# Attention and experts in one kernel: the first expert's early slots filled from six batches instead of seven

## The chip, the core and the metric

The kernel runs on one core of a Trainium2 chip. The metric is the device time of one execution in microseconds (us).

## What is computed

Eight batches of 576 tokens go through block-causal attention (8 heads of 64), and the result, 4608 rows of 512, goes through a mixture of eight experts. Each token is served by the one expert with the largest logit.

```python
scores = where(block(i) >= block(j), q @ k.T / 8, -1e9)
x      = softmax(scores) @ v                  # (8, 8, 576, 64) -> (4608, 512)
logits = x @ w_gate                           # (4608, 8)
e      = argmax(logits); g = softmax(logits)[e]
out[i] = g[i] * (relu(x[i] @ w1[e]) @ w2[e])  # w1: 512 x 1024, w2: 1024 x 512
```

## The kernel before

**Attention.** The work is cut into 32 pairs of heads, four to a batch. Pairs go through a software pipeline: a hand-written string, `ORDER`, lists the steps of one turn, each with a lag, and turn `t` runs step `name:lag` for pair `t - lag`. Scores are made with lag 2, transposes and products with V with lag 3, and with lag 4 the folds `F1`, `F2`, `F0` (L291, L297) that turn the pair's output into rows and gate logits, and the scalings `X1`, `X2` (L305, into the row tile `xt`), `Y1`, `Y2`, `Y0` (L312, L315). The last turn is turn 35, and only pair 31's lag 4 is left in it. Two folds share one PSUM bank, so `F2` needs `X1` and `Y1` done.

**Loads.** SP issues each pair's `qd`, `kd`, `v` (L96 to L98) one turn ahead of GpSimd's scaling `q<-qd` (L104, step `pQ`), which stands on GpSimd ahead of the scaling `p<-p,rs` (L205, step `Z`) of the pair two before it. Each turn PE waits for that `p` at the transpose `pt..t` (L228).

**Routing.** When a batch's four pairs are done, `Router.batch` runs as a generator: at each `z` in `ORDER` one step of it (two for batch 6). It ranks the tokens with matmuls, stores the rows to `xd` in DRAM (`rows`, L512 and L517) and queues in `late` five scatters that write token numbers into the table `tab` (L658). Each `y` of `ORDER`, two to a turn, takes one to four jobs off `late`. Where `late` is empty, a `y` takes a job off `todo` instead: the split of the first expert's w1 into `high` and `low`.

**The hand-over.** Three slots of 128 rows (`EARLY`) of the first expert are filled before routing has ended. After batch 6 the kernel reads the first three columns of the table (`first`, L632) and gathers their rows from `xd` into `xg[0..2]` (L674). `first_slot` then transposes slot 0 (L1207, between `F1` and `F2` of the last turn) and multiplies it with w1 (L1217) beside the rest of the last pair. Batch 7's columns 0 to 383 are stored by `part` as soon as three pairs are scaled, columns 384 to 511 after the last pair.

**Experts.** A critical section (L1026) begins when every transfer under way has landed. In it the engines follow hand-written programs with semaphores. DVE places batch 7's tokens (L649 to L653), prepares weights, and computes in `slots` (L696 to L713) which expert each slot serves; then come `high` (L1047) and `low` (L1053), the split of the weights, and PE's second layer `second_pe` (L934). SP loads the next weights and GpSimd gathers slot 3 (L794, L798) once `slots` is done.

Of the kernel before, what the change touches and what calls it, by code (L numbers as in the profile page):

```python
# [17 lines left out]
P = 128  # L18
# [20 lines left out]
class Attention:  # L39
# [8 lines left out]
    def __init__(self, ctx, tc, ident, qT, kT, vt, w_gate):  # L48
# [19 lines left out]
        self.small_bank, self.at = (None, None), {}  # L68
        self.used = {}
# [233 lines left out]
    def op_X(self, m, n):  # L303
        out = self.out(m // 4)[0][:, 2 * n - 2 : 2 * n, P * (m % 4) : P * (m % 4) + P]
        self.nc.vector.tensor_mul(  # L305
            out.rearrange("p i (j d) -> p i j d", d=D),
            self.rows(m, n)[:, :, 0:P].rearrange("p i (j d) -> p i j d", d=D), self.scaled(m, n, D),
        )

# [41 lines left out]
    def run(self, order, sink, part, other, then):  # L351
# [9 lines left out]
        for turn in range(self.M + last):  # L361
            for name, lag in order:
# [18 lines left out]
                if name[0] in "XY":  # L381
                    left[m // 4] -= 1
                    if left[m // 4] == 5:
                        part(m // 4, self.xs[m // 4][0])
# [51 lines left out]
EARLY = 3  # L436


class Router:
# [6 lines left out]
    def __init__(self, cp, tp, sp, tc, B, xd, tab, ident):  # L446
# [14 lines left out]
        for b in range(B):  # L461
# [28 lines left out]
            for c in range(self.ntok - S, self.ntok + 1, P)  # L490
        ]

        self.sums = [tp.tile([P, 2, E + 4], F32, tag=f"sum{i}", name=f"sum{i}") for i in range(2)]
        for t in self.sums:
            nc.gpsimd.memset(t[:, :, 0:4], 0.0)
        self.meta = {
            k: tp.tile(shape, dt, tag=k, name=k)
            for k, shape, dt in (
                ("cnti", [P, E], I32), ("each", [P, 2, E], I32), ("le", [P, 2, E], F32), ("prod", [P, 3, E], F32),
                ("n", [P, 2], F32), ("s", [P, 3], F32), ("si", [P, 2], I32), ("e8", [P, 1], I32),  # L500
# [5 lines left out]
    def rows(self, b, xt, x0, c0, c1):  # L506
# [12 lines left out]
        if b == self.B - 1:  # L519
            for m in put:  # L520
                self.keep_apart(m, 0)

# [6 lines left out]
    def batch(self, b, xt, x0, lg):  # L529
# [55 lines left out]
        if b >= self.B - 2:  # L585
# [24 lines left out]
        nc.sync.dma_start(self.xd[b * S : b * S + 64, GATE : GATE + 1], g[0:64, 4:5])  # L610
# [17 lines left out]
        if b == self.B - 2:  # L628
# [3 lines left out]
            self.late.append(lambda: nc.sync.dma_start(self.first, self.tabv[:, 0:EARLY]))  # L632
# [24 lines left out]
    def scatter(self, b, i, posi):  # L657
# [8 lines left out]
        if b < self.B - 1:  # L666
            for other in self.scatters:
                self.tc.declare_no_dep(put.ins, other.ins, reason="other rows")
            self.scatters.append(put)
        return put  # L670
# [10 lines left out]

    def next_late(self):

        for _ in self.late[: 1 if len(self.late) <= 5 else 4]:
            self.late.pop(0)()
        if len(self.late) == EARLY + 1:
            self.late.pop(0)()

    def slots(self, cnt, do):
# [3 lines left out]
        cnti, each, le, prod, n, s, si, e8, off, col, row = self.meta.values()  # L693
        a, c = self.sums
# [14 lines left out]
        do(v.tensor_sub(s[:, 0:1], self.part, s[:, 0:1]))  # L709
# [6 lines left out]
class Experts:  # L716
# [9 lines left out]
    def __init__(self, ctx, tc, ident, w1, w2, out, router, high, low):  # L726
# [26 lines left out]
        self.py = [b("py0"), b("py1")]  # L753

# [12 lines left out]
    def run(self):  # L767
# [258 lines left out]
        with tc.tile_critical():  # L1026
# [56 lines left out]
            self.router.slots(cnt, do)  # L1083
# [54 lines left out]
def attention_moe_kernel(ctx, tc, qT, kT, vt, w_gate, w1, w2, out):  # L1138
# [16 lines left out]
    with ExitStack() as actx:  # L1155
# [21 lines left out]
        def sink(b, xt, x0, lg):  # L1177
# [7 lines left out]
            if b == B - 2:  # L1185
# [3 lines left out]
            return router.batch(b, xt, x0, lg), 2 if b == B - 2 else 1  # L1189

        def part(b, xt):
            if b == B - 1:
                router.rows(b, xt, None, 0, 3 * P)
# [54 lines left out]
```

## Time and profile before

| what | value |
|---|---|
| median of three runs | 887.78 us (886.81 to 889.24) |
| the profiled execution, its own time | 886.42 us |
| its span on the core | 884.6 us |
| PE busy in the span | 841.5 us (95%) |
| DVE, ACT, GpSimd busy | 401.7, 459.5, 393.9 us |
| mean granted TensorE clock | 0.986 of full |

The span is counted from the first instruction to the last; some 1.8 us of the profiled execution lie around it. Times in rows are microseconds from the span's start. A turn of attention takes some 11 us, and attention fills the span up to about 387 us.

### The profile page before, as it was taken

How to read it: one execution, taken by the hardware profiler on the slowest of the kernel's cores; microseconds unless marked ns; L12 is line 12 of the kernel's file. 1: busy time of each engine (PE TensorE's matmuls, PEld its weight loads, DVE VectorE, ACT ScalarE, POOL GpSimd, SP SyncE). 2: the span in 40 equal slices, each digit the busy share in tenths (PEclk: the TensorE clock that was granted, in tenths of full speed). 3: DMA queues.
4: the chain of work that ended last, by engine and by line, in shares of the span. 5: the costliest groups of instructions: out<-in, count | busy, mean ns of one | idle time of the engine just before them, and what ended most of it. 6: DMA issues, size and time to landing. Idle time of an engine off the chain costs nothing.

```text
span 884.6 us, 15857 instructions
## 1 busy us (share of the span) xinstructions
PE 841.5 (95%) x4936; PEld 633.7 (72%) x4936; DVE 401.7 (45%) x1142; ACT 459.5 (52%) x1155; POOL 393.9 (45%) x392
## 2 busy tenths in 40 slices
PE   4999999999999999947999999999999999999994
PEld 3666666666666666636888888888888888888882
DVE  3667777767777777519804300045547352000000
ACT  3777777777777777514343443334433444334431
POOL 4122344444444323216655544455656655454541
PEclk9999999999999999979999999999999999999997
DMA  5228526273626261324733411125645531111110
GB/s 188 81 91 183 142 91 167 91 163 95 153 93 147 93 146 53 85 53 146 271 104 90 177 44 49 49 71 181 232 141 159 206 109 49 48 39 34 49 49 28
DMA packets 45043, 98.14 MB, mean 111 GB/s; under 512 B 7517, under 2 KB 10845, under 8 KB 44958
## 3 DMA queue, kind: packets, MB, share of 16 engines
q1 hardware_dynamic: 37438, 77.07, 30.2%
q0 software_dynamic: 7520, 19.97, 6.8%
q8 instruction: 49, 0.80, 0.4%
q14 instruction: 36, 0.29, 0.1%
HBM read 76.76 MB, written 20.79 MB: 110 GB/s over the span
## 4 chain that ended last, share of the span: by engine, by line
PE 89%; DMA 4%; DVE 3%; ACT 1%; issue 1%; POOL 1%; SPq 0%; POOLq 0%; DVEq 0%; ACTq 0%
PE py L934 24%; PE ph L855 22%; PE o L262 11%; PE ya L161 6%; PE xa L161 4%; PE pt L896 4%; PE o L297 3%; DMA xd<-xt 2%; PE px L816 2%; PE o L291 1%; DMA tab<-toks,posi 1%; PE o L150 1%; ACT pb L192 1%; DMA out<-y,idx 1%; DVE rc L651 1%
## 5 line engine op out<-in xcount | busy, mean ns | idle before, releaser
L934 PE MATMUL py<-w,low 128*128 (+1 forms) x912 | 232.9, 405 | 2.6 <-DVE w L1047 2.3
L934 PEld LDWEIGHTS py<-w,low 128*128 128x128 f32 x912 | 167.4, 190 | 38.7 <-DVE w L1047 2.7
L855 PE MATMUL ph<-w,xh 128*128 (+1 forms) x576 | 149.6, 392 | 0.9 <-ACT xf L829 0.9
L104 POOL TENSOR_SCALAR q<-qd 128x640 f32<-128x640 f32 x32 | 57.9, 1810 | 190.6 <-PE o L150 120.1
L1047 DVE CAST w<-raw 128x1024 fp32r<-128x1024 f32 x59 | 49.1, 881 | 193.6 <-PE ph L855 141.3
L855 PEld LDWEIGHTS ph<-w,xh 128*128 128x128 f32 x576 | 108.1, 188 | 24.9 <-ACT xf L829 1.1
L888 ACT ACTIVATE h<-ph 128x512 f32<-128x512 f32 x74 | 44.3, 599 | 146.6 <-PE ph L855 146.6
L916 POOL TENSOR_TENSOR low<-hf,low 128x512 fp32r<-128x512 f32 x74 | 101.1, 1366 | 36.7 <-ACT hf L910 36.7
L835 POOL TENSOR_TENSOR xl<-xf,xh 128x512 fp32r<-128x512 f32 x38 | 50.6, 1332 | 104.0 <-ACT xf L829 103.9
L1053 DVE TENSOR_TENSOR w<-raw,w 128x1024 fp32r<-128x1024 f32 x60 | 80.3, 1399 | 0.0
L855 PE MATMUL ph<-w,xl 128*128 (+1 forms) x288 | 77.5, 391 | 1.3 <-POOL xl L835 1.3
L906 ACT CAST low<-pt 128x512 fp32r<-128x512 f32 x76 | 45.8, 602 | 59.4 <-PE pt L896 56.6
L192 ACT ACTIVATE pb<-ya,neg 128x320 f32<-128x320 f32 (+2 forms) x96 | 50.1, 525 | 48.2 <-DVE neg L177 48.1
L954 POOL DMA_INDIRECT out<-y,idx x35 | 40.0, 1144 | 66.1 <-ACT y L948 66.1
L161 PE MATMUL ya<-kd,q 64*128 64x192 f32 (+2 forms) x192 | 61.8, 457 | 2.7 <-ACT pb L192 2.7
L855 PEld LDWEIGHTS ph<-w,xl 128*128 128x128 f32 x288 | 54.0, 188 | 13.5 <-POOL xl L835 1.7
L948 ACT ACTIVATE y<-py,xg 128x512 f32<-128x512 f32 x38 | 26.2, 689 | 71.8 <-PE py L934 71.8
L161 PE MATMUL yb<-kd,q 64*128 64x192 f32 (+2 forms) x192 | 61.8, 457 | 0.0
L658 POOL DMA_INDIRECT tab<-toks,posi x40 | 42.3, 1058 | 27.0 <-DVE run L625 19.6
L910 ACT COPY hf<-pt 128x512 f32<-128x512 f32 x76 | 46.4, 611 | 8.9 <-POOL low L916 8.6
L192 ACT ACTIVATE pb<-yb,neg 128x192 f32<-128x192 f32 (+2 forms) x96 | 49.8, 526 | 0.2 <-DVE neg L177 0.2
L798 POOL DMA_INDIRECT xg<-xd,idx x37 | 44.1, 1191 | 10.9 <-POOL idx L794 10.9
(937 smaller groups left out, 1641.6 us busy)
## 6 DMA issues: line engine op xcount, KB each, us to landing
raw<-w SPq DMA_DIRECT2D x60, 512.0 KB, 5.5
qd<-qT SPq DMA_DIRECT2D x32, 352.0 KB, 3.2
v<-vt SPq DMA_DIRECT2D x32, 352.0 KB, 4.4
kd<-kT SPq DMA_DIRECT2D x32, 288.0 KB, 3.9
xd<-xt SPq DMA_DIRECT2D x7, 1026.0 KB, 9.4
xg<-w SPq DMA_DIRECT2D x8, 256.0 KB, 8.5
xd<-xg SPq DMA_DIRECT2D x4, 256.5 KB, 12.0
xd<-x SPq DMA_DIRECT2D x8, 128.0 KB, 4.2
```

The source lines that it names most:

```text
L104: self.nc.gpsimd.tensor_scalar(q, self.raws[m][0][:, 0 : 512 + P], 0.125, None, ALU.mult)
L161: ins = mm(out, q[r, 128 * (i - 1) : 128 * i], k[r, o : o + n], start=True, stop=True, skip_group_check=True)
L192: ins = self.nc.scalar.activation(dst, src, AF.Exp, bias=self.neg[m][:, c : c + 1], scale=1.0, accum_out=self.sums[m][:, c : c + 1])
L262: self.nc.tensor.matmul(out[r], self.raws[m][2][:, slot], self.ph[m, bank][:, c0:c1], start=t in (0, 5), stop=t in (4, 5), skip_group_chec ...
L835: pool.tensor_sub(self.xl, self.xf, self.xh).then_inc(sem["xp"], 1)
L855: m = pe.matmul(self.ph[f], x[:, P * k : P * k + P], weights(k, f, part), start=start and k == 0, stop=stop and k == 3,)
L906: act.copy(self.hh[t % 2][:, f], self.pt[f]).then_inc(sem["ha"], 1)
L910: act.copy(self.hf, self.pt[f]).then_inc(sem["ha"], 1)
L916: engine.tensor_sub(self.hl[t % 2][:, f], self.hf, self.hh[t % 2][:, f]).then_inc(sem["hp"], 1)
L934: m = pe.matmul(self.py[t % 2], h[:, c // 4, P * (c % 4) : P * (c % 4) + P], wf[:, bass.ds(off + (base + 512 * c), 512)], start=n == 0, st ...
L1047: copy(hi, raw[m % nr]).then_inc(sem["wh"], 1)
L1053: dve.tensor_sub(lo, raw[m % nr], hi).then_inc(sem["wd"], 1)
```

## The change

Three things are done. **(1)** The early slots take tokens of batches 0 to 5 (`LATE = 2`): the counting matmuls, `lack`, the read of `first` and the three gathers follow batch 5 instead of batch 6. The gathers are declared free of the rows of batches 6 and 7, and the scatters of batch 6 free of the read of `first`. Batch 6 is routed at one step for each `z`. `next_late` takes one job per `y`. Since a slot may point at a row of the last two batches that is not yet written, nine writes of zeros (and one row) go to `xd` after batch 0 instead of four (and 65 rows). What is left of `todo` is issued when batch 5 ends instead of batch 6. **(2)** `X1`, `X2` of the last pair are declared free of the store `part`, which reads other columns of the same tile. **(3)** `slots` keeps its running values in a PSUM bank (`few`) and sums over experts by a product with a triangle of ones and one reduction, in place of three shifted adds in SBUF.

```diff
+LATE = 2
 class Router:
         self.zeros = [
             (xd[c : min(c + P, self.ntok + 1)], self.xg[0][0 : min(P, self.ntok + 1 - c)])
-            for c in range(self.ntok - S, self.ntok + 1, P)
+            for c in range(self.ntok - LATE * S, self.ntok + 1, P)
         ]
...
+        self.upto = tp.tile([P, E, E], F32, tag="upto", name="upto")
+        nc.gpsimd.memset(self.upto, 1.0)
+        nc.gpsimd.affine_select(out=self.upto, in_=self.upto, compare_op=ALU.is_ge, fill=0.0, ...)
...
 def batch(self, b, xt, x0, lg):
-        if b >= self.B - 2:
+        if last or b == self.B - LATE - 1:
             mm(total, self.ones, self.run[:, b], start=True, stop=False, skip_group_check=True)
...
-        if b == self.B - 2:
+        if b == self.B - LATE - 1:
             yield
             c = self.run[:, b + 1, 0:1]
             v.scalar_tensor_tensor(c, lack, float(EARLY), c, ALU.min, ALU.add)
-            self.late.append(lambda: nc.sync.dma_start(self.first, self.tabv[:, 0:EARLY]))
+            self.late.append(self.read_first)
             self.late += [lambda t=t: self.gather(t) for t in range(EARLY)]
...
 def next_late(self):
-        for _ in self.late[: 1 if len(self.late) <= 5 else 4]:
-            self.late.pop(0)()
-        if len(self.late) == EARLY + 1:
-            self.late.pop(0)()
+        self.late.pop(0)()
...
 def op_X(self, m, n):
+        for other in self.stored.get(m, ()):
+            self.tc.declare_no_dep(ins.ins, other.ins, reason="other columns")
...
-    def slots(self, cnt, do):
+    def slots(self, cnt, do, bank):
-        a, c = self.sums
+        a, le = (bank[:, 2 * E * i : 2 * E * i + 2 * E].rearrange("p (a e) -> p a e", a=2) for i in range(2))
+        s = bank[:, 4 * E : 4 * E + 3]
...
-        do(v.tensor_copy(a[:, :, 4:], each))
-        for k in (1, 2, 4):
-            do(v.tensor_add(c[:, :, 4:], a[:, :, 4:], a[:, :, 4 - k : 4 - k + E]))
-            a, c = c, a
-        do(v.tensor_scalar(le, a[:, :, 4:], self.part, None, ALU.is_le))
+        do(v.tensor_copy(a, each))
+        do(v.tensor_mul(sums, a[:, :, None, :].to_broadcast([P, 2, E, E]), self.upto[:, None].to_broadcast([P, 2, E, E])))
+        do(v.tensor_reduce(a, sums, AX.X, ALU.add))
+        do(v.tensor_scalar(le, a, self.part, None, ALU.is_le))
...
-        do(v.tensor_sub(s[:, 0:1], self.part, s[:, 0:1]))
+        do(v.tensor_scalar(s[:, 0:1], s[:, 0:1], self.part, -1.0, ALU.subtract, ALU.mult))
...
 def sink(b, xt, x0, lg):
-            if b == B - 2:
+            if b == B - LATE - 1:
                 while todo:
                     todo.pop(0)()
-            return router.batch(b, xt, x0, lg), 2 if b == B - 2 else 1
+            return router.batch(b, xt, x0, lg), 1
```

How the order of instructions changes on GpSimd at the hand-over, from pair 30's scaling on (`posi5`, `posi6` are batches 5 and 6, `p031` is pair 31's scaling, `sxl` belongs to slot 0). Before:

```order
L205 TENSOR_SCALAR p030_4485<-p030_4485,rs30_4483 128x64
L658 DMA tab_58<-toks_131,posi6_4691 43008x1 x4
L205 TENSOR_SCALAR p031_4618<-p031_4618,rs31_4616 128x64
L658 DMA tab_58<-toks_131,posi6_4691 43008x1
L674 DMA xg0_173<-xd_57,first_172 128x513
L674 DMA xg1_174<-xd_57,first_172 128x513
L674 DMA xg2_175<-xd_57,first_172 128x513
L1210 TENSOR_TENSOR sxl_4851<-oT_4852,sxh_4850 128x512
```

and with the change:

```order
L668 DMA tab_58<-toks_131,posi5_4186 43008x1
L206 TENSOR_SCALAR p030_4488<-p030_4488,rs30_4486 128x64
L686 DMA xg0_173<-xd_57,first_172 128x513
L686 DMA xg1_174<-xd_57,first_172 128x513
L206 TENSOR_SCALAR p031_4631<-p031_4631,rs31_4629 128x64
L686 DMA xg2_175<-xd_57,first_172 128x513
L668 DMA tab_58<-toks_131,posi6_4749 43008x1 x5
L1224 TENSOR_TENSOR sxl_4854<-oT_4855,sxh_4853 128x512
```

Two gathers now stand ahead of pair 31's scaling, and batch 6's five scatters behind the last gather, where four of them stood ahead of that scaling.

The other place is SP's queue after batch 0, where the zeros are written ahead of the first weights (`xg1` to `xg3`) and the loads of pair 8. `DMAHW0` to `DMAHW7` are the semaphores that SP's transfers take in turn: a row that waits for one waits until the transfer eight rows ahead of it has landed. Before:

```order
L1180 DMA xd_57<-xg0_173 128x513 [waits DMAHW3_49]
L1180 DMA xd_57<-xg0_173 128x513 [waits DMAHW4_49]
L1180 DMA xd_57<-xg0_173 128x513 [waits DMAHW5_49]
L1180 DMA xd_57<-xg0_173 128x513 [waits DMAHW6_49]
L1180 DMA xd_57<-xg0_173 65x513 [waits DMAHW7_49]
L1165 DMA xg1_174<-w1 128x512 [waits DMAHW0_49]
L1165 DMA xg2_175<-w1 128x512 [waits DMAHW1_49]
L1165 DMA xg3_176<-w1 128x512 [waits DMAHW2_49]
L96 DMA qd8_904<-qT 128x704 [waits DMAHW3_49,PE_49,Pool_49]
L97 DMA kd8_905<-kT 128x576 [waits DMAHW4_49]
L98 DMA v8_906<-vt 128x704 [waits DMAHW5_49]
```

and with the change, from the sixth write of zeros (five like it stand ahead) on:

```order
L1195 DMA xd_57<-xg0_173 128x513 [waits DMAHW0_49]
L1195 DMA xd_57<-xg0_173 128x513 [waits DMAHW1_49]
L1195 DMA xd_57<-xg0_173 128x513 [waits DMAHW2_49]
L1195 DMA xd_57<-xg0_173 128x513 [waits DMAHW3_49]
L1195 DMA xd_57<-xg0_173 1x513 [waits DMAHW4_49]
L1180 DMA xg1_174<-w1 128x512 [waits DMAHW5_49]
L1180 DMA xg2_175<-w1 128x512 [waits DMAHW6_49]
L1180 DMA xg3_176<-w1 128x512 [waits DMAHW7_49]
L97 DMA qd8_907<-qT 128x704 [waits DMAHW0_49,PE_49,Pool_49]
L98 DMA kd8_908<-kT 128x576 [waits DMAHW1_49]
L99 DMA v8_909<-vt 128x704 [waits DMAHW2_49]
```

Pair 8's loads, which stood behind the first, second and third write of zeros by their semaphores, now stand behind the sixth, seventh and eighth.

## Rows read from the trace of the kernel before

**Rows 1.** Waits of PE over the whole span: us in total, times, longest.

```profile
PE sa L1207 <- DMA xg<-xd,first: 8.0, 1, 8.0
...
PE px L816 <- SPq L1026: 3.5, 1, 3.5
...
PE py L934 <- DVE w L1047: 2.3, 1, 2.3
...
PE pt31t L228 <- POOL p L205: 0.5, 1, 0.5
```

**Rows 2.** The chain that ended last, 370 to 428 us: start, us, what.

```profile
370.80 6.89 DMA tab<-toks,posi
...
380.19 3.33 DMA xg<-xd,first
...
387.75 8.54 DMA xd<-xt
...
424.74 2.81 PE py L934 x12
```

**Rows 3.** PE's timeline: first fold of turn 34, of turn 35, slot 0's transposes.

```profile
367.09 0.66 PE L297 MATMUL o<-fold,oT 128*128 128x144 f32 x4
...
374.82 0.76 PE L297 MATMUL o<-fold,oT 128*128 128x144 f32 x4 [0.57 <-ACT oT L269]
383.56 1.11 PE L1207 MATMUL sa<-ident,xg 128*128 128x128 f32 x4 [7.98 <-DMA xg<-xd,first]
```

**Rows 4.** DVE's timeline: the last scaling of turns 34 and 35, and pair 31's X1.

```profile
370.05 0.29 DVE L312 COPY x<-o 64x144 f32<-64x144 f32 x1
...
377.63 0.43 DVE L305 TENSOR_TENSOR xt<-o,rs 128x256 f32<-128x256 f32 x1 [3.10 <-DMA xd<-xt]
...
386.78 0.29 DVE L312 COPY x<-o 64x144 f32<-64x144 f32 x1
```

**Rows 5.** The page's groups: the scatters on GpSimd, mean ns of one.

```profile
L658 POOL DMA_INDIRECT tab<-toks,posi x40 | 42.3, 1058 | 27.0 <-DVE run L625 19.6
```

**Rows 6.** SP's timeline: when pair 8's qd and v were issued.

```profile
74.39 0.33 SPq L96 DMA_DIRECT2D qd<-qT  x1
...
78.35 0.33 SPq L98 DMA_DIRECT2D v<-vt  x1
```

**Rows 7.** DMA issues of the whole span: KB each, median us to landing.

```profile
qd<-qT SPq DMA_DIRECT2D x32, 352.0 KB, 3.2
```

**Rows 8.** DMA issues between 60 and 82 us: KB each, median us to landing.

```profile
qd<-qT SPq DMA_DIRECT2D x2, 352.0 KB, 5.7
```

**Rows 9.** GpSimd's timeline in turn 9: pair 8's q, pair 6's p.

```profile
85.47 1.81 POOL L104 TENSOR_SCALAR q<-qd 128x640 f32<-128x640 f32 x1 [8.07 <-PE o L150]
88.32 0.44 POOL L205 TENSOR_SCALAR p<-p,rs 128x64 f32<-128x64 f32 x1 [1.04 <-ACT ph6k L243]
```

**Rows 10.** PE's timeline in turn 9: the transpose that needs pair 6's p.

```profile
90.56 0.27 PE L228 MATMUL pt6t<-ident,p 128*64 128x128 f32 x1
```

**Rows 11.** DVE's timeline in and behind `slots`.

```profile
408.35 3.18 DVE L703 TENSOR_SCALAR le<-sum,part 128x16 f32<-128x16 f32 x1
...
412.40 1.12 DVE L708 CAST si<-s 128x2 int32<-128x2 f32 x1
...
414.61 1.90 DVE L1047 CAST w<-raw 128x1024 fp32r<-128x1024 f32 x3
```

**Rows 12.** GpSimd's timeline at the same place.

```profile
410.20 1.29 POOL L916 TENSOR_TENSOR low<-hf,low 128x512 fp32r<-128x512 f32 x1
412.19 1.29 POOL L916 TENSOR_TENSOR low<-hf,low 128x512 fp32r<-128x512 f32 x1 [0.70 <-ACT hf L910]
...
416.27 1.11 POOL L798 DMA_INDIRECT xg<-xd,idx  x1 [0.32 <-POOL idx L794]
```

**Rows 13.** PE's timeline: the first 24 matmuls of the second layer.

```profile
416.56 7.30 PE L934 MATMUL py<-w,low 128*128 128x512 f32 x24 [2.30 <-DVE w L1047]
```

**Rows 14.** The window 416.5 to 418: busy PE, PEld, DVE, ACT, POOL; PEclk, DMA share, GB/s.

```profile
416.50:418.00 1.50, 1.44 (x3) 1.16 (x4) 1.47 (x3) 0.00 (x0) 0.88 (x1) 0.50 0.87 248
```

More of the change, by code (lines that the diff above doesn't have):

```diff
@@ L383, in run @@
                     if left[m // 4] == 5:
-                        part(m // 4, self.xs[m // 4][0])
+                        self.stored[4 * (m // 4) + 3] = part(m // 4, self.xs[m // 4][0])
                     if left[m // 4] == 0:
@@ L489, in __init__ @@
             (xd[c : min(c + P, self.ntok + 1)], self.xg[0][0 : min(P, self.ntok + 1 - c)])
-            for c in range(self.ntok - S, self.ntok + 1, P)
+            for c in range(self.ntok - LATE * S, self.ntok + 1, P)
         ]
-        self.sums = [tp.tile([P, 2, E + 4], F32, tag=f"sum{i}", name=f"sum{i}") for i in range(2)]
-        for t in self.sums:
-            nc.gpsimd.memset(t[:, :, 0:4], 0.0)
+        self.upto = tp.tile([P, E, E], F32, tag="upto", name="upto")
+        nc.gpsimd.memset(self.upto, 1.0)
+        nc.gpsimd.affine_select(
+            out=self.upto, in_=self.upto, compare_op=ALU.is_ge, fill=0.0, base=0, pattern=[[1, E], [-1, E]],
+            channel_multiplier=0,
+        )
         self.meta = {
@@ L609, in batch @@
         self.rows(b, xt, x0, 0, RW)
[L610 removed]
+        m = nc.sync.dma_start(self.xd[b * S : b * S + 64, GATE : GATE + 1], g[0:64, 4:5])
+        if b >= self.B - LATE:
+            self.keep_apart(m, 0)
         yield
@@ L669, in scatter @@
             self.scatters.append(put)
+            if b >= self.B - LATE:
+                self.tc.declare_no_dep(put.ins, self.closed.ins, reason="other columns")
         return put
@@ L680, in gather, with read_first @@
         self.keep_apart(m, 1)
+    def read_first(self):
+        self.closed = self.nc.sync.dma_start(self.first, self.tabv[:, 0:EARLY])
     def next_late(self):
-        for _ in self.late[: 1 if len(self.late) <= 5 else 4]:
-            self.late.pop(0)()
-        if len(self.late) == EARLY + 1:
-            self.late.pop(0)()
-    def slots(self, cnt, do):
+        self.late.pop(0)()
+    def slots(self, cnt, do, bank):
         v = self.nc.vector
-        cnti, each, le, prod, n, s, si, e8, off, col, row = self.meta.values()
-        a, c = self.sums
+        cnti, each, prod, n, sums, si, e8, off, col, row = self.meta.values()
+        a, le = (bank[:, 2 * E * i : 2 * E * i + 2 * E].rearrange("p (a e) -> p a e", a=2) for i in range(2))
+        s = bank[:, 4 * E : 4 * E + 3]
         do(v.tensor_scalar(cnti, cnt, float(SL - 1), None, ALU.add))
@@ L1082, in run @@
                 dve.tensor_copy(self.w[:, 0, 0, o], self.high[:, o]).then_inc(sem["wh"], 2)
-            self.router.slots(cnt, do)
+            self.router.slots(cnt, do, self.bank)
             dve.sem_inc(sem["me"], 1)
@@ L1184, in sink @@
                 here.append(b)
-            if b == B - 2:
+            if b == B - LATE - 1:
                 while todo:
                     todo.pop(0)()
-            return router.batch(b, xt, x0, lg), 2 if b == B - 2 else 1
+            return router.batch(b, xt, x0, lg), 1
         def part(b, xt):
-            if b == B - 1:
-                router.rows(b, xt, None, 0, 3 * P)
+            return router.rows(b, xt, None, 0, 3 * P) if b == B - 1 else []
         def other():
```

13 lines of the change are left out of this document (8 added, 5 removed).

## The prediction

> **What bounds the kernel now.** I read the page first: PE is busy for 841.5 of 884.6 us, so only what PE waits for can be won or lost. PE's waits come next [rows 1]: the longest by far is 8.0 us in front of slot 0's transposes, on the gather of the first expert's rows; 3.5 us go to the start of the critical section, 2.3 to the weight splits behind `slots`, 0.5 to pair 31's `p`. Third, the chain [rows 2] says what makes that gather late: batch 6's last scatter lands 6.89 us after 370.80, then the table is read, then the gather needs 3.33 us and ends at 383.5. Behind it comes the store of the last columns, 8.54 us from 387.75, and the critical section opens when it lands at 396.29. So two links in a row set the hand-over: routing of batch 6, and the last store.
>
> **Part 1 and 2, the hand-over.** In the last turn the first fold starts at 374.82 and the last scaling, whose end releases the store, ends at 386.78 + 0.29 = 387.07 [rows 3, 4]. The same steps one turn earlier take from 367.09 to 370.34, 3.25 us. The difference, 9.0 us, holds the wait for the gather (7.98), `X1`'s wait for another store (it begins at 377.63 after 3.10 us; the fold was done at 375.6), and transposes and folds at a low clock (1.11 us where the same kind takes 0.66). For the last turn to run like the one before it, both waits must go: with the gather early but `X1` still held until 377.63, only about 7 us would go. By the new order both go: the gather of slot 0 stands behind pair 30's scaling, a turn ahead of its use, and needs 3.33 us; `X1` has no DMA left to wait for.
>
> Batch 6's scatters used to stand ahead of pair 31's `p`, which cost PE 0.5 us [rows 1]; now one gather issue stands between, and I count the 0.5 as won. Together **9.5 us**: the last scaling ends at 377.5, the last store lands at about 386.8.
>
> What is late next? The five scatters now come after pair 31's gather, once batch 6's positions are known, by the order just behind turn 34's second `X2`, some 370.3 [rows 4]. At 1.06 us each with a gap [rows 5] the last is issued near 377 and, at the 6.89 us seen before [rows 2], lands by 384, ahead of the store. They also stand ahead of slot 0's `sxl` on GpSimd, which PE needs only after two groups of matmuls and the ranking. Their price is zero, and up to 3 us if the store's landing is drawn out by them or by batch 6's rows, which now leave a turn's third later, close to `part`. Slot 0's matmuls themselves have cover: PE stood idle for 3.5 us at the critical section [rows 1], so their end is not what it waits for.
>
> Moved work with no price: six tiny counting matmuls go from batch 6 to batch 5; batch 6's routing steps spread over two turns, in which DVE has idle time; the rest of `todo` goes to GpSimd earlier, where it idles more than half of the span; the three declarations cost nothing.
>
> **The zeros.** Nine writes of 256 KB go out where four did, and by the order pair 8's `qd` now waits for the sixth to land instead of the first. Before, `qd` was issued at 74.39 and `v`, two writes on, at 78.35 [rows 6]: 1.98 us for a write. So `qd` is issued at 74.39 + 5 x 1.98 = 84.3, and lands after 3.2 us (the median of all) to 5.7 (in this busy stretch) [rows 7, 8]: 87.5 to 90.0. GpSimd then needs 1.81 us for `q` and 0.44 for `p` [rows 9] behind it in its queue, and PE wants that `p` at 90.56 [rows 10]. It comes at 89.8 to 92.3: a new stall of 0 to 1.8 us in turn 9, which attention, with PE at 100%, never gives back. I take **1.0 us lost**; if the loads also queue behind the last three writes and the first weights, it is up to 5. The `q` itself, `kd` and `v` are used a turn later and stay covered.
>
> **Part 3, `slots`.** The row shows `le`, 16 elements a partition, taking 3.18 us and ending at 411.53, 0.04 us behind GpSimd's `low` (411.49); the cast `si` takes 1.12 us and ends 0.04 behind the next `low` (413.48) [rows 11, 12]. The four steps between them take 0.22 each. So a one-source step from SBUF to SBUF sits out GpSimd's work, and the others don't. With both in PSUM I take 2.96 + 0.90 = 3.9 us off; product and reduction in place of three adds are about even. From `le` on, eleven steps of 0.22 end near 410.8 instead of 414.5.
>
> Then the three casts `high` (0.63 each) meet GpSimd's two `low`: done between 412.7 and 414.8. PE has been free since 416.56 - 2.30 = 414.26 [rows 13], so it starts at 414.3 to 414.8 and wins about 2.1 us. The 24 matmuls took 7.30 us there, where a dozen takes 2.81 [rows 2], because the clock stood at half (0.50) behind the wait [rows 14]; with the wait gone I expect full clock and 5.6 us, so 1.7 more. But then slot 3's rows come due: their gather began at 416.27 [rows 12], 1.8 us behind the end of `slots`, and cannot start much before 413.48 + 1.8 = 415.3, and an early gather landed after 3.33 us [rows 2]; beside the weight loads I allow 5. PE would reach it at 420.1 and gets it at 418.6 to 420.3. I take **2.8 us** won of 3.8, with 0.5 (casts held, clock still falls) and 4 as ends.
>
> Not all of `slots` is freed: `off`, `e8` and `row` still go from SBUF to SBUF. They come at about 410, inside the `low` that ends at 411.49. If they wait, `slots` ends at 412.1 and the casts at 414.0 to 415.4. The Trainium skill ("SBUF — State Buffer", section "SBUF: two separate sides") says that DVE and GpSimd share a pair of ports under an exclusive lock, so that a DVE step in a two-port mode is blocked for a whole GpSimd instruction; "VectorE: DVE Perf Modes", section "Why PSUM operands drop a tier", says that a PSUM operand rules that mode out. The trace agrees for `le` and `si`; by the same rule the three left over would wait, and the sum would win 2.0 there instead of 2.8. No row shows such a step with one element a partition under a GpSimd instruction, so I keep the larger value.
>
> **The sum.** 9.5 - 1.0 + 2.8 = 11.3 us. The profiled execution took 886.42, so 875.1 for one like it; it lies 1.36 below the median of the three runs (887.78), and against that the forecast is **876.5 us**.
>
> **The rivals.**
> - *The zeros cost 5 us.* For it: in the old trace the transfers keep the engines busy until pair 8's loads are in. Against: the spacing of 1.98 us. 876.5 + 4.0 = 880.5. Chance 0.15.
> - *`slots` wins nothing*: the leftovers or the casts wait for GpSimd, or slot 3's gather binds, and the clock falls all the same. 876.5 + 2.3 = 878.8. Chance 0.12.
> - *The last store lands late*, behind `part`, batch 6's rows and five scatters, which were all done before. For it: three transfers now share the stretch; against: the data are small. 876.5 + 3 = 879.5. Chance 0.08.
> - *Slower.* The writes of zeros hold SP's queue so long that turns 9 and 10 run dry. With s us for a write the stall is 74.39 + 5s + 5.7 + 2.25 - 90.56 = 5s - 8.2; the 12.3 us won elsewhere and 2.7 more (0.3%) are used up from s = 4.6. At s = 5 the stall is 16.8, 4.5 us more than is won: 892.3. The trace shows 1.98, so chance 0.02.
> - *An extra slot.* If the first expert had under 384 tokens in batches 0 to 5, padding would make a slot more, some 12 us (468 us from 416.56 to the end, over 38 slots): 888.5, no change. Against: from the reference's inputs it has 192 + 128 + 576 = 896 there. Chance 0.03, with everything else that eats up the whole gain.
>
> **How the numbers follow.** The forecast with its own bounds (872.5 to 879) has 0.60. 0.3% is about what a measurement of this kernel tells from no change, 2.7 us. Faster by more than that: the forecast and the first three rivals, 0.95; within it 0.03; slower 0.02. The range runs from 871.5 (no stall at the zeros, 4 us at `slots`, a point more at the hand-over) to 882 (two of the first three rivals at once).
>
> **What would show it.** Right: no wait of PE at slot 0's transposes and none at the last `pt..t`; critical section opened 9 to 10 us earlier; `le` and `si` near 0.2 us, the second layer's first 24 matmuls in under 6 us; a new wait of PE on `p` in turn 9 of 0 to 2 us. Wrong: a wait for `first` or a gather left on GpSimd ahead of pair 31's `p`; `X1` still ending at a store; the last store landing over 9.5 us after its issue; PE waiting in turns 9 to 11 for loads by more than 5 us.

## The result, and the profile after

The changed kernel takes 880.13 us in the median of eight runs (875.76 to 883.50), the kernel before 887.39 in eight runs beside them (885.07 to 890.53). The ratio is 0.9908, with an interval of 0.9881 to 0.9936: faster by about 1%. A second set of runs gave 874.34 against 885.64, ratio 0.9881 [0.9857, 0.9906] (experiment e1). The execution profiled after, the fastest of its eight, took 875.76 us, with a span of 874.0; the one before took 886.42 and 884.6. The two profiles are 10.6 us of span apart.

PE's waits over the whole span of the changed kernel (us in total, times, longest; beside them stand only those of the first and second turns, two of 0.7 and 0.6 us that are shown further down, and some under 0.7 us that both kernels share):

```profile
PE px L831 <- issue: 4.3, 1, 4.3
...
PE pt6t L229 <- POOL p L206: 2.2, 1, 2.2
...
PE bank L585 <- DVE oh L569: 0.9, 1, 0.9
```

Against [rows 1], the 8.0 us at slot 0's transposes are gone, and so are the 0.5 us on pair 31's `p`; the splits' 2.3 us are 0.7. New are 2.2 us on pair 6's `p`, 0.9 us on the ranking inside slot 0's matmuls, and 0.6 us on slot 3's gather. The wait for the critical section grew from 3.5 to 4.3. Two waits that the kernel before had just behind the section's start, 1.3 us for GpSimd's `xl` and 0.9 us for ACT's `xf`, are gone too.

**The last turn.** PE's and DVE's timeline of the changed kernel (start, us, engine, line, what, idle time ahead and what ended it): first fold, slot 0's transposes, second fold; `X1` and the last scaling:

```profile
376.29 0.76 PE L298 MATMUL o<-fold,oT 128*128 128x144 f32 x4 [0.57 <-ACT oT L270]
376.89 0.60 PE L1221 MATMUL sa<-ident,xg 128*128 128x128 f32 x4
377.76 0.73 PE L298 MATMUL o<-fold,oT 128*128 128x144 f32 x4 [0.27 <-DVE lg L318]
...
377.09 0.42 DVE L306 TENSOR_TENSOR xt<-o,rs 128x256 f32<-128x256 f32 x1 [1.09 <-PE o L298]
...
379.35 0.29 DVE L315 COPY x<-o 64x144 f32<-64x144 f32 x1
```

From the fold to the end of the last scaling it is 3.35 us (376.29 to 379.64), where [rows 3, 4] had 12.25. `X1` now ends its wait at PE's fold, not at a store. GpSimd's timeline shows the gathers that made this possible, the first and second (at 361.60) ahead of pair 31's `p`, and the five scatters of batch 6 behind the third:

```profile
360.26 1.03 POOL L686 DMA_INDIRECT xg<-xd,first  x1 [0.39 <-issue]
...
369.68 0.44 POOL L206 TENSOR_SCALAR p<-p,rs 128x64 f32<-128x64 f32 x1 [7.14 <-ACT ph31b L244]
370.32 1.01 POOL L686 DMA_INDIRECT xg<-xd,first  x1 [0.19 <-issue]
372.85 1.01 POOL L668 DMA_INDIRECT tab<-toks,posi  x1 [1.52 <-DVE run L635]
...
378.05 0.98 POOL L668 DMA_INDIRECT tab<-toks,posi  x1 [0.31 <-issue]
```

In the chain that ended last, the last store is still the link into the critical section, and a little longer than in [rows 2] (8.54):

```profile
380.31 9.03 DMA xd<-xt
```

Only the first part of it is data. For the five microseconds ahead of its landing at 389.34 the DMA engines move nothing (columns: us, busy PE, PEld, DVE, ACT, POOL; PEclk, DMA share, GB/s), and before it was the same from 391 to 396. What fills that time the profiles don't show.

```profile
384.00:389.00 5.00, 2.24 (x10) 1.49 (x8) 0.00 (x0) 0.67 (x2) 0.00 (x0) 1.00 0.00 0
```

**Turn 9.** SP's, GpSimd's and PE's timeline: the zeros, the first weights, pair 8's `qd`; pair 8's `q`, pair 6's `p`, the transpose that wants it.

```profile
65.19 9.58 SPq L1195 DMA_DIRECT2D xd<-xg  x10
75.98 5.53 SPq L1180 DMA_DIRECT2D xg<-w  x3
83.31 0.33 SPq L97 DMA_DIRECT2D qd<-qT  x1
...
90.73 1.81 POOL L105 TENSOR_SCALAR q<-qd 128x640 f32<-128x640 f32 x1 [13.24 <-DVE g L648]
92.52 0.44 POOL L206 TENSOR_SCALAR p<-p,rs 128x64 f32<-128x64 f32 x1
...
93.02 0.30 PE L229 MATMUL pt6t<-ident,p 128*64 128x128 f32 x1 [2.21 <-POOL p L206]
```

`qd` was issued at 74.39 before [rows 6] and goes out 8.9 us later; `q` starts 5.3 us later than in [rows 9]. The DVE step named ahead of `q` was done long before; in e1 the same row begins at 89.37 and names the transfer `qd`.

**Behind the critical section.** PE's timeline: the first transposes, the second layer's first 24 matmuls, slot 3's transposes.

```profile
390.55 1.12 PE L831 MATMUL px<-ident,xg 128*128 128x128 f32 x4 [4.31 <-issue]
...
408.27 5.84 PE L949 MATMUL py<-w,low 128*128 128x512 f32 x24 [0.74 <-DVE w L1062]
...
414.68 0.65 PE L831 MATMUL px<-ident,xg 128*128 128x128 f32 x4 [0.57 <-DMA xg<-xd,idx]
```

Before, the first of these rows stood at 397.46, the last at 423.70. So the 10.6 us divide as 6.91 up to the critical section's first transposes, 2.11 from there to slot 3's (26.24 us became 24.13), and 1.6 in the steady rest, which nothing in the prediction accounts for.

The same place on DVE (`few` is the PSUM bank; then the first and last of the three steps left in SBUF, of 0.15 us each, and the weight splits) and on GpSimd:

```profile
402.76 0.24 DVE L717 TENSOR_SCALAR few<-few,part 128x16 f32<-128x16 f32 x1
...
403.88 0.16 DVE L722 CAST si<-few 128x2 int32<-128x2 f32 x1
...
404.52 0.15 DVE L725 TENSOR_SCALAR off<-si 128x1 int32<-128x1 int32 x1
...
404.90 0.15 DVE L727 TENSOR_SCALAR row<-n 128x1 int32<-128x1 f32 x1
405.20 3.01 DVE L1062 CAST w<-raw 128x1024 fp32r<-128x1024 f32 x3
...
402.24 1.30 POOL L850 TENSOR_TENSOR xl<-xf,xh 128x512 fp32r<-128x512 f32 x1
403.49 1.29 POOL L931 TENSOR_TENSOR low<-hf,low 128x512 fp32r<-128x512 f32 x1
405.47 1.59 POOL L931 TENSOR_TENSOR low<-hf,low 128x512 fp32r<-128x512 f32 x1 [0.69 <-ACT hf L925]
...
408.70 1.65 POOL L813 DMA_INDIRECT xg<-xd,idx  x1 [0.45 <-POOL idx L809]
```

The steps that took 3.18 and 1.12 us [rows 11] take 0.24 and 0.16, and both run while GpSimd works (`xl` and the first `low`). The three splits, which are still held by the second `low`, take 3.01 instead of 1.90.

### The profile page after: what moved, and what is told of

The parts are those of the page before. It is cut to its first block, busy times and chain, and to the rows that moved or that the text cites. A ratio compares the mean times of both kernels' runs of the same rounds, so it can differ in the third digit from the quotient of the medians.

```text
span 874.0 us, 15861 instructions
## 1 busy us (share of the span) xinstructions
PE 838.9 (96%) x4936; PEld 632.9 (72%) x4936; DVE 399.4 (46%) x1141; ACT 459.7 (53%) x1155; POOL 397.1 (45%) x392
## 4 chain that ended last, share of the span: by engine, by line
PE 86%; DMA 5%; issue 2%; POOL 2%; ACT 2%; DVE 1%; SPq 1%; POOLq 0%; DVEq 0%; ACTq 0%
PE py L949 23%; PE ph L870 22%; PE o L263 10%; PE ya L162 6%; PE xa L162 4%; PE pt L911 4%; PE o L298 3%; PE px L831 2%; DMA xd<-xg 2%; PE o L292 1%; DMA xd<-xt 1%; ACT pb L193 1%; DMA qd<-qT 1%; DMA xg<-xd,idx 1%; POOL tab L668 1%
## 5 line engine op out<-in xcount | busy, mean ns | idle before, releaser
L949 PE MATMUL py<-w,low 128*128 (+1 forms) x912 | 229.9, 401 | 0.8 <-DVE w L1062 0.7
L931 POOL TENSOR_TENSOR low<-hf,low 128x512 fp32r<-128x512 f32 x74 | 102.9, 1391 | 35.5 <-ACT hf L925 35.5
L1068 DVE TENSOR_TENSOR w<-raw,w 128x1024 fp32r<-128x1024 f32 x60 | 83.1, 1445 | 0.0
```

What stands on the lines that cost most here:

```text
L931: engine.tensor_sub(self.hl[t % 2][:, f], self.hf, self.hh[t % 2][:, f]).then_inc(sem["hp"], 1)
L949: m = pe.matmul(self.py[t % 2], h[:, c // 4, P * (c % 4) : P * (c % 4) + P], wf[:, bass.ds(off + (base + 512 * c), 512)], start=n == 0, st ...
L1068: dve.tensor_sub(lo, raw[m % nr], hi).then_inc(sem["wd"], 1)
```

## The experiments

Each is compared with runs of the kernel before on the same chip: 885.64 us for e1 to e4, 885.16 for e5 to e8, 885.05 for e9 to e12. Differences between experiments are of medians; between sets they carry the 0.6 us by which the medians of before differ.

**e1, the changed kernel again**, unchanged.

> The changed kernel once more, for a second trace. Theory (what differs between executions lies in the experts' part, whatever the kernel): the third row transpose, slot 3's, starts again at 414.7 us (414 to 415.5), and only the stretch from there to the end differs from the 459.3 us of the first trace, by as much as the execution's own time does. Rival (the change itself is drawn differently each time: the clock at the critical section, the last store, the loads): the slot-3 transposes start 2 us or more away from 414.7 and the stretch behind them stays within 0.7 us of 459.3.

Measured: 874.34 us (872.55 to 877.72), ratio 0.9881 [0.9857, 0.9906]; span 871.0. From slot 3's transposes (411.58) to the end it is 459.4 us, against 459.3 in the first profile: the experts' part does not differ between these two executions, so that theory is wrong (in e3, whose program is the same there, it was 461.2). What differs lies ahead: the wait in turn 9 is 0.9 instead of 2.2 us, the last store takes 8.11 instead of 9.03, and the clock behind the critical section falls later.

**e2, the zeros spread** over batches 0, 1 and 2.

```diff
-            if b == 0:
-                for rows, zero in router.zeros:
-                    nc.sync.dma_start(rows, zero)
+            for rows, zero in router.zeros[4 * b : 4 * b + 4]:
+                nc.sync.dma_start(rows, zero)
+            if b == 0:
```

> The ten writes of zeros go out four after batch 0, four after batch 1, two after batch 2, instead of all after batch 0. Theory: PE's 2.2 us wait for pair 6's p in turn 9 goes, nothing takes its place, and the time is 2.2 us below the changed kernel's (1.5 to 2.5). Rival: the writes hold loads wherever they stand, waits of PE on a p or a load come up behind batches 1 and 2, and the time stays within 0.7 us of the changed kernel's. If all ten had a price of 5 us, as one rival of the prediction had it, 4 us or more would come back.

Measured: 871.93 us (871.53 to 873.22), ratio 0.9846 [0.9824, 0.9867], 2.4 us under e1. SP's timeline shows pair 8's `qd` where it was before the change (74.39 in [rows 6]), and PE has no wait on `p` left, nor another in its place:

```profile
64.78 2.48 SPq L1194 DMA_DIRECT2D xd<-xg  x4
...
74.53 0.33 SPq L97 DMA_DIRECT2D qd<-qT  x1
```

So the stall of turn 9 is the zeros' and can be had back. How much that is in time is less sure: the medians say 2.4 us, the traces of the kernels with all zeros behind batch 0 show stalls of 0 to 2.2, and the profiled execution of e2, with a span of 871.5, was no shorter than that of e1 (871.0). Slot 0's transposes start at 374.52 here; in the profiles with part 1 and all zeros behind batch 0 they start at 375.13 to 376.89 (the first, e1, e4, e5, e10, e12), and at 378.38 in e3. The narrow range of these runs did not hold in later kernels with the same edit (e9 reached 878.47); what makes single runs longer stays open.

**e3, `X1` held again** (part 2 taken out: the two lines of `declare_no_dep` in `op_X`).

> The changed kernel without part 2: the last pair's X1 and X2 wait for the store of batch 7's columns 0 to 383 again. Theory: that store is issued near 372.4 and lands 7.4 us later, so X1 starts near 379.8 instead of 377.1, the last scaling and the start of the critical section move by 2.7 us, and the time is 2 to 3.5 us above the changed kernel's. Rival (something else, scatters or slot 0's matmuls, sets the start of the critical section): the time moves by less than 0.7 us.

Measured: 878.03 us (876.49 to 883.33), ratio 0.9918 [0.9899, 0.9937], 3.7 us over e1. DVE's timeline, and PE's wait behind it:

```profile
381.36 0.43 DVE L306 TENSOR_TENSOR xt<-o,rs 128x256 f32<-128x256 f32 x1 [3.87 <-DMA xd<-xt]
```

```profile
PE o L298 <- DVE lg L316: 3.0, 1, 3.0
```

With the gather out of the way, `X1` waits for the store of the first columns, and the second fold for `X1`'s bank: the second wait of the row, as the prediction had it, 3.0 us where 0.3 are left with part 2. The difference is the 2.7 us of the theory; the 3.7 of the medians lie a little over its 3.5. The spans of the two profiles can't be compared beyond that: in e3 PE also waited 2.2 us for slot 3's gather, the stall of turn 9 was 1.9 us, and behind that stall the clock fell for a while, as the window of 90 to 100 us shows (columns: us, busy PE, PEld, DVE, ACT, POOL; PEclk, DMA share, GB/s); in e1 it stood at 1.00 there.

```profile
90.00:100.00 10.00, 8.09 (x44) 4.17 (x45) 4.77 (x22) 4.88 (x17) 2.23 (x2) 0.83 0.32 117
```

**e4, the old `slots`** in the changed kernel (part 3 taken out).

```diff
-        do(v.tensor_mul(sums, a[:, :, None, :].to_broadcast([P, 2, E, E]), self.upto[:, None].to_broadcast([P, 2, E, E])))
-        do(v.tensor_reduce(a, sums, AX.X, ALU.add))
-        do(v.tensor_scalar(le, a, self.part, None, ALU.is_le))
+        for k in (1, 2, 4):
+            do(v.tensor_add(c[:, :, 4:], a[:, :, 4:], a[:, :, 4 - k : 4 - k + E]))
+            a, c = c, a
+        do(v.tensor_scalar(le, a[:, :, 4:], self.part, None, ALU.is_le))
```

> The changed kernel with the slots function of the kernel before (SBUF, three shifted adds). Theory: the step le takes about 3 us and si about 1 us again, slots ends 3.9 us later, PE waits 2.5 us or more for the weight casts, the first 24 matmuls of the second layer take 7.3 us again at half clock, and the time is 2.5 to 4 us above the changed kernel's. Rival (the casts and slot 3's gather bind anyway): less than 0.7 us.

Measured: 877.06 us (875.32 to 882.63), ratio 0.9920 [0.9892, 0.9949]: 2.7 us over e1, and 8.6 under before for parts 1 and 2 alone. PE's timeline shows the wait for the splits back, but not the long second layer of [rows 13]; then slot 3's transposes and, 35 slots on, the last ones:

```profile
407.21 5.88 PE L944 MATMUL py<-w,low 128*128 128x512 f32 x24 [2.32 <-DVE w L1057]
412.93 0.60 PE L826 MATMUL px<-ident,xg 128*128 128x128 f32 x4
...
847.63 0.60 PE L826 MATMUL px<-ident,xg 128*128 128x128 f32 x4
```

So only a part of the 2.7 us lies in front of slot 3. From 412.93 to 847.63 it is 434.70 us, 12.420 for each of 35 slots. Before it was 434.71 (423.70 to 858.41), but in the changed kernel 433.41 (414.68, as shown above, to 848.09):

```profile
848.09 0.60 PE L831 MATMUL px<-ident,xg 128*128 128x128 f32 x4
```

That is 12.383 a slot, and 1.3 us in all. The engines do the same work there. What differs in the two programs is where the experts' tiles lie in SBUF: part 3 changed the small tiles ahead of them, so that all of them, the weights `w` first, moved up by 480 bytes in each partition. Four runs test that.

**e5, the old `slots`, tiles moved by 32 bytes.**

```diff
+        self.pad = t("pad", [P, 8])
         self.w = t("w", [P, 2, 4, 4096], F32R)
```

> The changed kernel with the old `slots` (as in e4), and 32 unused bytes a partition ahead of the experts' tiles: the weight tile `w` begins at byte 62272 of a partition (a multiple of 64) instead of 62240 (32 over one). Nothing else differs. In the profiles so far a slot of the steady part, from one set of row transposes to the next, takes 12.420 us in before and e4 and 12.383 in the changed kernel, e1, e2 and e3; the difference of 0.037 us lies in the second layer's matmuls. Theory, place of the tiles: the slot takes 12.38 here, the median comes out 1.3 us under e4's 877.06 (875.3 to 876.2), and the stretch from slot 3's transposes to the end is 1.3 us shorter than e4's 460.7. Rival, the old `slots` itself leaves something behind (another clock, another order of SP's and GpSimd's work): the slot takes 12.42, median 876.6 to 877.5.

Measured: 876.58 us (874.84 to 878.09), ratio 0.9906 [0.9893, 0.9919]. From 414.81 to 849.04 it is 434.23 us, 12.407 a slot: between the two. Of 12.38 and 12.42 neither came; the place has an effect, but one of 64 bytes is not the whole of it.

**e6, e2 with the same 32 bytes.**

> e2 (zeros spread over batches 0 to 2) with the same 32 bytes, which here take `w` from 62720 (a multiple of 64) to 62752 (32 over one). Theory, place of the tiles: a slot goes from 12.38 back to 12.42 us and the median from 871.93 to 873.0 to 873.6. Rival: 12.38 and 871.5 to 872.4, the place modulo 64 does not matter (then only a place further off, or something else in the new `slots`, does).

Measured: 874.25 us (873.57 to 876.92), ratio 0.9888 [0.9873, 0.9902]; from 411.26 to 846.01 it is 434.75 us, 12.421 a slot, with the new `slots`. The place theory holds for the slot: the longer one comes back by 32 unused bytes. The median lies 0.65 us over the 873.6 that the theory allowed.

**e9, e2 with 64 bytes** (`[P, 16]` in place of `[P, 8]`).

> e2 with 64 unused bytes ahead of the experts' tiles: `w` from 62720 (a multiple of 256) to 62784 (64 over a multiple of 128). So far, by place: 12.381 us a slot at 62720, 12.406 at 62272 (e5, also 64 over a multiple of 128; old `slots`), 12.420 at 62240 and 62752 (32 over). Theory, the place of the experts' tiles alone sets the slot's time, by how far it is from a multiple of 128 bytes: 12.406 here, 0.9 us longer over 35 slots than e2, median 872.4 to 873.2. Rival, in e5 the old `slots` kept half of the difference: 12.38 here and 871.5 to 872.4.

Measured: 872.93 us (872.29 to 878.47), ratio 0.9880 [0.9851, 0.9909]; 12.408 a slot.

**e10, e4 with 480 bytes** (`[P, 120]`), which puts all of the experts' tiles where the changed kernel has them.

> e4 (the changed kernel with the old `slots`) with 480 unused bytes ahead, so that every tile of the experts lies where it does in the changed kernel (`w` at 62720). Theory, the place alone: 12.381 us a slot, 1.3 us less than e4 over the experts' part, median 875.3 to 876.2; what is then left between this and e1 (874.34), 1.0 to 1.9 us, is what the new `slots` is worth by its own steps. Rival, the old `slots`: 12.406 as in e5, and 876.2 to 877.

Measured: 875.32 us (873.91 to 879.31), ratio 0.9896 [0.9871, 0.9921]; PE's timeline:

```profile
407.07 5.85 PE L945 MATMUL py<-w,low 128*128 128x512 f32 x24 [2.94 <-DVE w L1058]
412.76 0.60 PE L827 MATMUL px<-ident,xg 128*128 128x128 f32 x4
...
846.14 0.60 PE L827 MATMUL px<-ident,xg 128*128 128x128 f32 x4
```

433.38 us, 12.382 a slot, with the old `slots`: the place alone sets it. Together:

| first byte of `w` in a partition | over a multiple of 128 | kernels | us a slot |
|---|---|---|---|
| 62240, 62752 | 32 | before, e4; e6 | 12.420, 12.420; 12.421 |
| 62272, 62784 | 64 | e5; e9 | 12.407; 12.408 |
| 62720 | 0 | after, e2; e10 | 12.383, 12.383; 12.382 |

Which of the tiles it is was not tried; they all moved together, and the others lie at other remainders than `w`. Nor is 128 shown to be the period: the two places of a line lie 512 bytes apart, and only these three distances were tried.

Between e10 and e1, which differ by the steps of `slots` alone, 1.0 us is left; the two are of different sets, and their intervals overlap. DVE's and GpSimd's timelines of e10 also show another step waiting (the first of the three adds, the first product; then GpSimd's two `low`):

```profile
398.18 3.24 DVE L711 TENSOR_TENSOR sum<-sum 128x16 f32<-128x16 f32 x1
...
402.35 1.05 DVE L715 TENSOR_TENSOR prod<-le,each 128x16 f32<-128x16 f32 x1
...
400.08 1.30 POOL L927 TENSOR_TENSOR low<-hf,low 128x512 fp32r<-128x512 f32 x1
...
402.07 1.30 POOL L927 TENSOR_TENSOR low<-hf,low 128x512 fp32r<-128x512 f32 x1 [0.70 <-ACT hf L921]
```

Here these steps, with two sources in SBUF, end 0.04 and 0.03 us behind a `low`, where in before and e4 the adds took 0.18 each and `le` and `si` waited; in e10 `le` takes 0.24 and `si` 0.17. The old `slots` as a whole takes as long either way, 7.6 to 7.7 us.

**e7, filler matmuls** in e2: 16 more behind slot 0's first layer, into a PSUM tile that nothing reads, so that PE does not idle ahead of the critical section.

```diff
+            more = att.ps_t.tile([P, 512], F32, tag="pt", name="warm")
+            for k in range(16):
+                nc.tensor.matmul(more, xh[:, 0:P], high[:, 0:512], start=k == 0, stop=k == 15, skip_group_check=True)
```

> e2 with 16 more matmuls behind slot 0's first layer (into a PSUM tile that nothing reads), so that PE works on while it would wait for the critical section. In the changed kernel and e2 PE idles 3.7 to 4.3 us there and then runs the first transposes at half clock (1.12 us instead of 0.66), which ends ACT's copy and the low half of slot 0's hidden layer later, and with them the start of `slots`. My theory: at full clock `slots` begins about 1.4 us earlier, the weight splits and slot 3's gather follow it, and the median falls by 0.8 to 1.5 us from 871.93, to 870.4 to 871.1. Rival: GpSimd's scatters of batch 7 end later than that anyway, `slots` begins when it did, and nothing is won (871.5 to 872.4); first transposes at 0.66 all the same. Third: the added matmuls run past the landing of the last store and hold PE by 0.5 to 1 us (872.5 to 873).

Measured: 872.98 us (872.08 to 873.34), ratio 0.9861 [0.9847, 0.9875]; PE's timeline:

```profile
383.67 3.90 PE L1238 MATMUL warm<-high,sxh 128*128 128x512 f32 x16
388.71 0.66 PE L831 MATMUL px<-ident,xg 128*128 128x128 f32 x4 [1.14 <-issue]
...
405.69 5.85 PE L949 MATMUL py<-w,low 128*128 128x512 f32 x24 [0.20 <-DVE w L1062]
```

The third of the outcomes: the clock holds, but the chain now goes back to the fillers, the section opens 1.14 us behind the last of them, at 388.71 instead of e2's 387.63, and at the second layer nothing is left of it (405.69 against 405.36).

**e11, nine of them.**

> e7 with 9 added matmuls instead of 16. In e7 they ran from 383.67 to 387.57, the critical section opened 1.1 us later than in e2 (first transposes at 388.71 instead of 387.63), and full clock behind it gave the 1.2 us back. Nine end near 385.9, before the last store lands. My theory: first transposes at 387.6 again and at 0.66 us, the second layer's first matmuls some 0.7 to 1.1 us earlier than e2's 405.36, median 870.8 to 871.4. Rival: in the 1.7 us that PE still idles the clock falls as in e2, first transposes at 1.12, 871.5 to 872.4. Third: slot 3's gather takes back what is won before it (its wait grows from 1.0 to 2 us), 871.6 to 872.2 at full clock.

Measured: 872.60 us (872.17 to 872.99), ratio 0.9857 [0.9831, 0.9884]; PE's timeline:

```profile
383.63 2.26 PE L1238 MATMUL warm<-high,sxh 128*128 128x512 f32 x9
387.03 0.66 PE L831 MATMUL px<-ident,xg 128*128 128x128 f32 x4 [1.14 <-issue]
...
403.99 5.85 PE L949 MATMUL py<-w,low 128*128 128x512 f32 x24 [0.17 <-DVE w L1062]
...
411.00 0.65 PE L831 MATMUL px<-ident,xg 128*128 128x128 f32 x4 [1.16 <-DMA xg<-xd,idx]
```

The clock holds, and the section again opens 1.14 us behind the last filler. From the first transposes to the second layer it is 16.96 us (17.73 in e2), to slot 3's 23.97 (24.58): 0.77 us won by the clock and 0.6 left behind slot 3's gather. The medians don't show it (872.60 against 871.93 in another set, with intervals that overlap, where 870.8 to 871.4 was expected), so in time this is inconclusive.

**e8, part 2 alone** in the kernel before.

> The kernel before with part 2 alone (the last pair's `X1`, `X2` free of the store `part`). My theory: the hand-over is a row of two waits, and with slot 0's gather landing at 383.5 PE waits for that gather whatever `X1` does: the fold behind it cannot start earlier, so 0 to 0.4 us faster than before (wait on slot 0's transposes stays at 7.5 to 8 us). Together with e3 (part 2 taken away from the changed kernel: +3.7 us by medians) that makes the two parts worth more together than apart. Rival, the parts add up: part 2 is worth its 3 us here too, and the median lies 2.5 to 3.5 us under before.

Measured: 885.69 us (883.08 to 888.49), ratio 1.0009 [0.9995, 1.0023]; PE's waits:

```profile
PE sa L1210 <- DMA xg<-xd,first: 7.5, 1, 7.5
```

Nothing, as my theory had it: behind the gather `X1` has time to wait.

**e12, part 1 alone.**

> Part 1 alone: early slots from six batches with the nine writes of zeros, `X1` held by the store, old `slots`, tiles where they lie in before. By addition from e1, e3 and e4: 874.34 + 3.7 + 2.7 = 880.7, that is 4.5 us faster than before. Theory, part 3 acts behind the critical section and adds to the others: 879.9 to 881.5. Rival, `slots` and its follow-on waits depend on how the critical section is entered (a later, longer idle, another clock): outside that, 878 to 879.5 or 882 to 883.5. First transposes of the critical section at 394 to 395, slot 0's transposes without a wait, PE's wait for `lg` (3.0 us in e3) there again.

Measured: 880.59 us (879.34 to 883.31), ratio 0.9953 [0.9936, 0.9970]; PE's timeline:

```profile
379.60 1.30 PE L298 MATMUL o<-fold,oT 128*128 128x144 f32 x4 [3.87 <-DVE lg L316]
```

The sum from e1, e3 and e4 was 880.7. (The first transposes came at 391.83, ahead of the 394 expected.) So the parts stand thus, in us against before: part 2 alone 0.5 slower, which is no change; part 1 alone 4.5 faster; 1 and 2 8.6 (e4); 1 and 3 7.6 (e3); all 11.3 (e1); with the zeros spread, the fastest of them, 13.7 (e2).

## Why the prediction was right, and where a step failed

The forecast was 11.3 us: 875.1 for an execution like the one profiled, which took 875.76, and 876.5 against the median. The medians gained 7.3 us (880.13) and, in e1, 11.3. The first lies inside the range but 1.1 us over the forecast's own bounds (872.5 to 879), and that the second meets the forecast to a tenth is partly luck, as the terms show. The profile after is of the fastest of eight executions, so it can't show what the others lost. In most kernels the longer executions have the lower mean granted clock (875.76 us at 0.990 and 883.50 at 0.987 in the first set; 875.32 at 0.993 and 882.63 at 0.985 in e4); which of their waits costs it stays open.

- **Hand-over, 9.5 us: right, by its mechanism and size.** The last scaling ends at 379.64 instead of 387.07, 7.43 us earlier, and 2.21 us of stall in turn 9 lie ahead of it: 9.6. Both waits had to go: part 2 alone wins nothing (e8), part 1 without part 2 leaves PE 3 to 3.9 us of wait behind `X1` (e3, e12). The 0.5 us on pair 31's `p` came too. By medians parts 1 and 2 together won 8.6 us (e4), where 9.5 - 1.0 = 8.5 was forecast. One sign did not come: the critical section's first transposes stand 6.91 us earlier, not 9 to 10; the stall of turn 9 and the longer landing of the store took the other 2.7.
- **Scatters behind the gather: price zero held.** They were issued from 372.85 to 378.05 where 377 was forecast for the last, and no wait of PE ends at them.
- **The last store: a little under-priced.** Its landing took 9.03 us instead of 8.54. Over the profiles of the changed kernel and the experiments it took 7.5 to 9.0, so the rival of a late store (over 9.5) did not come, and the 0.5 us are within chance.
- **Zeros, 1.0 us: right on average, its upper end too low.** `qd` was issued at 83.31, forecast 84.3. But `q` began 7.4 us later, where 3.2 to 5.7 were allowed for the landing, and the stall was 2.2, over the 1.8. The last writes were still landing while `qd` was under way (`kd` and `v`, which wait for the seventh and eighth, went out at 85.77 and 87.59), so the loads did queue, as the text had it for its worst case, though not to 5 us. In the seven profiles with all zeros after batch 0 (the first, e1, e3, e4, e5, e10, e12) it was 2.2, 0.9, 1.9, 0.9, 0.3, none and 0.5, in the mean 0.96. Two things move it: in e5 and e10 PE already came 0.8 to 1.0 us late to turn 9, which takes up as much of the wait, and in e3 the clock fell behind the stall, which cost about 1.5 us more (pair 9's `q` at 100.82 instead of 99.32 in the first profile). In e2 the stall is gone.
- **`slots`, 2.8 us: the sum came out, the working only in part.** Its first step held: 3.9 us off, 7.69 to 3.76. One reading under it was wrong, that only one-source steps from SBUF to SBUF sit out GpSimd's work. In before the four steps between `le` and `si` ran from 411.57 to 412.36, nearly all in the gap between the two `low` (411.49 to 412.19), so they had nothing to wait for; in e10 an add and a product with two SBUF sources did wait, 3.24 and 1.05 us. The gain does not hang on it, because the change gave these steps a PSUM operand too: the products at 403.25 and 403.46 took 0.17 us each beside `xl` and `low`.
  The leftovers did not wait: in the changed kernel `off` ran at 404.52 inside a `low` that lasted from 403.49 to 404.78, in 0.15 us, and in e1 all three (401.26 to 401.79, 0.15 each) inside one from 400.75 to 402.05. The Trainium skill's rule of the exclusive lock ("SBUF — State Buffer", section "SBUF: two separate sides"), by which the sum had 2.0, is not borne out for these steps, as I applied it. The Trainium skill ("VectorE: DVE Perf Modes", section "Side-by-side: where the cycles go for N=2048 bf16") ties the two-port mode to the outermost dimension that is not one, which must be even, or equal in source and destination; of a step without such a dimension that section says nothing. For the weight splits the lock's rule agrees (3.01 us for three beside a `low`, 1.90 in [rows 11] without one).
  The second step failed: the 1.7 us from the clock. I put the 7.30 us of [rows 13] down to the wait ahead of it. Between the two profiles the gain came (7.30 to 5.84), but e4 and e10 have waits of 2.32 and 2.94 and run the 24 matmuls at full clock in 5.88 and 5.85. That loss belongs to some executions, not to the wait alone.
  The third, slot 3's gather, bounds as forecast (0.6 to 1.2 us of wait in the profiles with the new `slots`, 2.2 in e3), but by another link: it starts 1.64 us behind GpSimd's `low` (ending at 407.06), not 1.8 behind `slots` (405.05). What is won up to slot 3's transposes is 2.1 us in the profiles; by medians, without the place of the tiles, it is 1.0 (e10 against e1) to 1.4 (e4 against e1, 2.7 less 1.3), within the noise of either.
- **Not in the prediction: 1.3 us** from the place of the tiles, which made up for what the clock term lacked. So it is luck that part 3's 2.7 us by medians (e4 against e1) come so near to the forecast 2.8.
- **Not in the prediction: the clock behind the critical section.** There PE now waits 4.3 us instead of 3.5, and the first transposes run at the lower level, as the window of 390.5 to 392.5 us of the changed kernel shows (us, busy PE, PEld, DVE, ACT, POOL; PEclk, DMA share, GB/s):

```profile
390.50:392.50 2.00, 1.95 (x9) 1.95 (x10) 1.76 (x6) 0.79 (x2) 0.00 (x0) 0.50 0.25 36
```

Most of it is hidden, because PE had waited there before: for GpSimd's `xl`, which stands behind the scatters of batch 7 (1.3 us), and for `xf` (0.9); e11 shows what is not, 0.6 to 0.8 us.

The rivals: zeros at 5 us, `slots` at nothing, an extra slot (38 groups of transposes in both profiles) and the slower case did not come.

## What to carry to other kernels

Where two waits stand in a row on one path, price them together: each edit alone won 0 or 4.5 us, both 8.6. When work is moved ahead of other transfers in a queue, take the landing time of the load behind it from the busiest stretch and leave room above; a large write that nothing needs soon can be split over several turns at no cost that these runs show. When a step is seen to wait for another engine, ask which of its neighbours would wait if the two met a little earlier: in e10 it was the adds and not `le`. And before a gain is put down to a step, look at the steady part too: a tile that a change adds or drops can move all tiles behind it.

## What the runs showed of the hardware

- **The place of a tile in SBUF.** The same steady work takes 12.383, 12.407 or 12.420 us a slot, as the weight tile `w` begins 0, 64 or 32 bytes over a multiple of 128 in a partition and the other tiles of the experts move with it: 1.3 us of 433 over 35 slots. Five places were tried; which tile counts, and whether 128 is the period, is not shown. I had expected nothing of it.
- **TensorE's clock after idle time.** After 1.14 us of idle time at the critical section it stayed at 1.00 (e7, e11). After 2.89, 3.15 and 3.54 us it also did (e12, e4, before), but after 2.94 us (e8), 2.99 (e10) and 3.13 to 4.31 us (e1, e2, e3, e5, e6, e9, after) it fell to 0.50, that is from 2.4 to 1.2 GHz. Behind the wait for the splits it fell after 2.30 to 3.33 us in before, e5, e8 and e12, and stayed after 2.32 and 2.94 us in e4 and e10; behind waits of 0.74 us and less there it never fell. Ahead of slot 3 it fell after 2.16 us (e3). In turn 9 it fell after 1.91 us (e3) and not after 2.21 (after). The length of the wait alone does not decide it.
- **Small DVE steps beside GpSimd.** DVE's steps of one element a partition between SBUF tiles took 0.15 us under a `low` of 1.3 us (three of them in e1), where one-source steps of 16 and 2 elements had taken 3.18 and 1.12 [rows 11], and two-source steps of 16 elements took 3.24 and 1.05 in e10. With an operand in PSUM, `le` and `si` took 0.24 and 0.16 beside the same work of GpSimd.
- **The tail of a store.** The last store, 256 KB, landed 9.03 us after its issue in the changed kernel; in the last five of them the DMA engines moved nothing (share 0.00 from 384 to 389 us). In before it was 8.54 us, with a share of 0.00 from 391 to 396.
